# Rows of about one KB in the loads, and 32 stationary columns on four column groups in the products of a with the state

## The chip, the cores and the metric

The kernel runs on one NeuronCore of a Trainium2 chip. The metric is device time in microseconds: the median of several executions, and beside it one execution that was taken with the hardware profiler. TensorE's engine is PE in the views (PEld is its weight loads), VectorE is DVE, ScalarE is ACT, GpSimd is POOL, SyncE is SP. Most transfers are issued by SP's queue, in the order in which they stand there.

## The reference, cut to what matters

```python
# r, k, v, w, a, b: (4, 8, 768, 40) float32; state: (4, 8, 40, 40)
for t in range(768):
    y[:, :, t] = einsum('bhd,bhde->bhe', rt, state)
    Sa = einsum('bhde,bhe->bhd', state, at)
    state = state * wt[:, :, None, :] - einsum('bhd,bhe->bhde', Sa, bt) + einsum('bhd,bhe->bhde', vt, kt)
x = y, as (4 * 768, 320)
h = maximum(x @ w_in, 0);  x = (h * h) @ w_out               # 320 -> 2048 -> 320
g = x @ w_gate;  x = (g / (1 + exp(-g)) * (x @ w_val)) @ w_out   # 320 -> 1536 -> 320
```

The five weight matrices come as float64.

## The kernel before, in words

The recurrence is done in chunks of 32 steps (`C`), 24 chunks per batch. A group g (48 of them) is one chunk of two batches, that is 16 (batch, head) states, eight on partitions 0 to 39 and eight on 64 to 103 (of 104, `EPAD`). `e_stage` (lines 761 to 790) loads a group's w, a, k and b (`WA`, printed as wakb or room) and builds decay products with scans on DVE; `x_stage` multiplies a and b products inside a chunk; `inverse` solves the triangular systems of a window of four groups with 30 small DVE operations, after its input went through DRAM (`xi`); `chain` (lines 924 to 1006) carries the state from chunk to chunk, in 24 steps of stages named u, s and t; `slot` (lines 1015 to 1092) makes the output y from k, c, z, S and y stages. Four slots are one block of 256 rows for the first MLP (`pair1`), whose products (lines 461 and 466, each float32 matrix as a high and a low fp32r part) run between the stages of the recurrence. The second MLP follows when the recurrence is over, after about 750 us.

The stage u sums two things in one PSUM bank: 32 products with 32 stationary columns (line 955), then 16 products of a with the state (line 961), each with 64 stationary columns that hold the two halves q of a, and 40 moving columns of the state:

```python
for p in range(2):
    s = 4 * (n % 2) + 2 * (n // 2) + p
    nc.tensor.matmul(quad(tag)[64 * p:64 * p + 64, u, n], AB[nas[u]][:, s].rearrange("e q t -> e (q t)"),
                     ST[u][:, s, 0:D], start=False, stop=u + n == 4)
```

TensorE is used in tiles (32x32, 64x64, 128x64, or the whole array); the planner calls that an operation's mode, and two of one mode may be put behind each other. Each of these float32 products stands in the trace as two records.

The weights of the first MLP are loaded by `conv` (lines 1237 to 1278) in 36 jobs through four buffers `cx` (one lies in the tile `room`), turned from float64 into float32 by ACT, DVE and POOL, and split. The last 64 of the 320 rows of w_in would fill only half the partitions, so four of the jobs (named hl jobs here) bring two column blocks of them at once, one onto partitions 0 to 63, one onto 64 to 127, in one transfer whose source is written with the block as its outermost dimension (lines 1169 to 1171):

```python
src = w[r0:r0 + 64, c.start:c.start + 512].rearrange("p (g n) -> g p n", g=2)
```

The order of the work on all engines is set when the program is built, by a planner (class `Plan`): every operation has a due time and a cost per engine, and the planner simulates the engines and writes each engine's instructions in the order of its simulation. While PE would be idle before 220 us of its own time, it puts in filler products (line 1288, tile `warm`). The order on an engine is fixed from then on, and an engine waits at each instruction for what it needs.

## Time and profile before

| | us |
|---|---|
| median of 3 executions | 1205.25 (1201.82 to 1207.41) |
| profiled execution, its own time | 1207.99 |
| its span, first to last instruction | 1206.2 |
| granted TensorE clock, mean over the span | 0.959 of full speed |
| PE busy | 1115.2 |

The span falls into a front of about 205 us in which the weights are brought in and the recurrence starts, a dense part to about 755 us in which the recurrence and the first MLP share PE, and the second MLP. The profiled execution is 2.74 us above the median. A time in a row is counted from the span's start.

### The profile page before, as it was taken

How to read it: one execution, taken by the hardware profiler on the slowest of the kernel's cores; microseconds unless marked ns; L12 is line 12 of the kernel's file. 1: busy time of each engine (PE TensorE's matmuls, PEld its weight loads, DVE VectorE, ACT ScalarE, POOL GpSimd, SP SyncE). 2: the span in 40 equal slices, each digit the busy share in tenths (PEclk: the TensorE clock that was granted, in tenths of full speed). 3: DMA queues.
4: the chain of work that ended last, by engine and by line, in shares of the span. 5: the costliest groups of instructions: out<-in, count | busy, mean ns of one | idle time of the engine just before them, and what ended most of it. 6: DMA issues, size and time to landing. Idle time of an engine off the chain costs nothing.

```text
span 1206.2 us, 42916 instructions
## 1 busy us (share of the span) xinstructions
PE 1115.2 (92%) x18622; PEld 1016.1 (84%) x18622; DVE 643.8 (53%) x1551; ACT 550.0 (46%) x1296; POOL 93.3 (8%) x118
## 2 busy tenths in 40 slices
PE   7486987999899998999898999999999999999997
PEld 6475877889898997989797989988888888888886
DVE  4775876666575574856464422355444343434433
ACT  6344875555465464655454445563322222222221
POOL 0221332001110101110000000000000000000000
PEclk9688888999899998999899999999999999999998
DMA  5645555555566565654243321533101010010000
GB/s 136 152 122 161 151 161 140 128 155 150 146 161 175 129 166 127 171 143 116 83 104 80 76 66 44 142 97 90 32 12 27 22 27 23 20 29 1 22 1 26
DMA packets 171394, 114.97 MB, mean 95 GB/s; under 512 B 104092, under 2 KB 147644, under 8 KB 171196
## 3 DMA queue, kind: packets, MB, share of 16 engines
q1 hardware_dynamic: 168470, 110.62, 35.1%
q8 instruction: 148, 2.42, 0.8%
q10 hardware_dynamic: 2726, 1.51, 0.5%
q14 instruction: 50, 0.41, 0.1%
HBM read 88.35 MB, written 23.72 MB: 93 GB/s over the span
## 4 chain that ended last, share of the span: by engine, by line
PE 78%; DMA 7%; DVE 5%; issue 4%; SPq 3%; ACT 2%; POOL 0%; DVEq 0%; ACTq 0%
PE ps L461 33%; PE ps L466 13%; PE ps L1479 10%; SPq L724 3%; PE ps L1058 3%; PE ps L1030 2%; PE ps L1039 2%; PE ps L961 2%; PE ps L803 2%; DMA ws<-f_moe_w_val 2%; PE ps L1073 2%; PE ps L1000 2%; PE ps L974 2%; PE ps L869 1%; PE ps L955 1%
## 5 line engine op out<-in xcount | busy, mean ns | idle before, releaser
L1471 DVE TENSOR_TENSOR gr<-ps,gr 128x512 f32<-128x512 f32 x144 | 99.5, 691 | 165.9 <-PE ps L461 84.3
L1152 ACT ACTIVATE ps<-ps 128x512 f32<-128x512 f32 x192 | 111.6, 581 | 108.8 <-PE ps L461 106.7
L466 PE MATMUL ps<-o1h,gh 128*128 128x320 f32 x384 | 132.9, 346 | 3.6 <-ACT gh L436 3.6
L466 PE MATMUL ps<-o1h,gl 128*128 128x320 f32 x384 | 123.2, 321 | 1.6 <-DVE gl L413 1.4
L436 ACT CAST gh<-gr 128x512 fp32r<-128x512 f32 x72 | 44.7, 621 | 174.1 <-DVE gr L1471 173.7
L466 PE MATMUL ps<-o1l,gh 128*128 128x320 f32 x384 | 121.9, 318 | 0.0
L461 PE MATMUL ps<-xh,w1h 128*128 128x256 f32 x384 | 117.9, 307 | 0.0
L461 PE MATMUL ps<-xl,w1h 128*128 128x256 f32 x384 | 110.9, 289 | 0.1
L461 PE MATMUL ps<-xh,w1l 128*128 128x256 f32 x384 | 110.6, 288 | 0.0
L1479 PE MATMUL ps<-o2h,gl 128*128 128x320 f32 x288 | 89.1, 309 | 0.1
L1479 PE MATMUL ps<-o2l,gh 128*128 128x320 f32 x288 | 88.9, 309 | 0.2 <-DVE o2l L1395 0.2
L1479 PE MATMUL ps<-o2h,gh 128*128 128x320 f32 x288 | 88.8, 308 | 0.2 <-ACT o2h L436 0.2
L413 DVE TENSOR_TENSOR gl<-ps,gh 128x512 fp32r<-128x512 f32 x96 | 65.5, 682 | 34.2 <-ACT gh L436 33.7
L466 PEld LDWEIGHTS ps<-o1h,gh 128*128 128x128 f32 x384 | 74.8, 195 | 8.0 <-ACT gh L436 4.5
L1468 ACT ACTIVATE gr<-ps 128x512 f32<-128x512 f32 x72 | 43.2, 600 | 80.9 <-PE ps L461 79.4
L466 PEld LDWEIGHTS ps<-o1h,gl 128*128 128x128 f32 x384 | 75.0, 195 | 4.1 <-DVE gl L413 3.9
L461 PEld LDWEIGHTS ps<-xh,w1h 128*128 128x128 f32 x384 | 75.2, 196 | 1.7
L461 PEld LDWEIGHTS ps<-xl,w1h 128*128 128x128 f32 x384 | 75.5, 197 | 0.4 <-DVE xl L1101 0.3
L466 PEld LDWEIGHTS ps<-o1l,gh 128*128 128x128 f32 x384 | 75.4, 196 | 0.1
L461 PEld LDWEIGHTS ps<-xh,w1l 128*128 128x128 f32 x384 | 75.0, 195 | 0.0
L1133 DVE TENSOR_TENSOR gl<-gr,gh 128x512 fp32r<-128x512 f32 x72 | 49.9, 693 | 46.8 <-ACT gh L436 46.8
L1288 PE MATMUL ps<-warm 128*128 128x256 f32 x284 | 48.8, 328 | 22.1 <-DVE ct L1219 13.9
(171 smaller groups left out, 2711.4 us busy)
## 6 DMA issues: line engine op xcount, KB each, us to landing
wakb<-in_wakb_dram SPq DMA_DIRECT2D x42, 422.5 KB
RB<-in_vr_e_dram SPq DMA_DIRECT2D x46, 208.0 KB
RH<-in_r_e_dram SPq DMA_DIRECT2D x90, 80.0 KB
cx<-in_moe_w_out_dram SPq DMA_DIRECT2D x21, 320.0 KB
room<-xt_d SPq DMA_DIRECT2D x36, 128.0 KB
cx<-in_moe_w_in_dram SPq DMA_DIRECT2D x15, 256.0 KB
xt_d<-yb SPq DMA_DIRECT2D x24, 160.0 KB
x_d<-room SPq DMA_DIRECT2D x24, 160.0 KB
```

The source lines that it names most:

```text
L413: nc.vector.tensor_sub(dst, full, hi.bitcast(F32))
L436: nc.scalar.copy(dst, src) if e == ACT else eng[e].tensor_copy(dst, src)
L461: nc.tensor.matmul(ps, w[:, c], x, start=(i == 0), stop=(i == len(seq_) - 1))
L466: nc.tensor.matmul(acc[t][:, :DM], g[:, half, ts], w[:, f, :], start=(f == 0 and i == 0), stop=(f == nf - 1 and i == 2),)
L724: o = att(cost, lambda e: queues[e].dma_start(dst(), src()), r, w, due=due, dma=dma, tag="dma")
L1058: nc.tensor.matmul(v[64 * q:64 * q + D, p, s], w, x, start=not kb, stop=bool(kb))
L1133: op({POOL: t_pool(512), DVE: t_dve(512)}, lambda e: eng[e].tensor_sub(gl[n], two["gr"][n], gh[n].bitcast(F32)), (("gr", n), ("gh", n)), ( ...
L1152: op({ACT: 0.478}, lambda e, f=f: nc.scalar.activation(P1[b], P1[b], f), (), (("p", b),), due=due, tag="relu")
L1288: nc.tensor.matmul(PS[:, b, 0:256].rearrange("p (a b) -> p a b", a=2), warm, warm[:, None, :].to_broadcast([128, 2, 128]), start=True, sto ...
L1468: op({ACT: 0.478}, lambda e: nc.scalar.activation(both(two["gr"]), two["pg"][b], AF.Sigmoid), (("pg", b),), (("gr", n),), tag="sig", **kw)
L1471: op({DVE: 0.602}, lambda e, q=q: nc.vector.tensor_mul(both(two["gr"]), two[q][b], both(two["gr"])), ((q, b),), (("gr", n),), tag="u" + q, ...
L1479: nc.tensor.matmul(ACC2[t][:, :DM], x[n][:, t // 2, c], y[:, f, :], start=(f == 0 and i == 0), stop=(f == nf - 1 and i == 2))
```

## The change

Four things are changed.
- In the stage u, each product of a with the state is cut in two: 32 stationary columns (one q) instead of 64, so 32 products instead of 16 per step, on four column groups of the array. The planner is told a cost of 1.0 instead of 1.35 for the stage, and that it leaves the array in 128x32 mode.
- The tiles into which wakb, RB, RH and cx are loaded get a gap of two elements between rows of about 1 KB, so that a row of 2 to 4 KB lands as two to four rows. For groups from 4 on, wakb, until now one transfer of 1040 columns, is now two (272 columns, and 3 x 256).
- The hl jobs' loads are now two transfers of 64 partitions each, without the outer dimension of two.
- The identity matrix is loaded into the tile UQ and copied by ACT into one fp32r tile that serves the fillers and the transposes.

```diff
+GAP = 2
-    ident = keep.tile([128, 128], F32, name="ident")
+    warm = keep.tile([128, 128], F32R, name="ident")
+    ident = warm.bitcast(F32)
...
+    def in_halves(x, n):
+        return x.rearrange("p (k c) -> p k c", k=2)[:, :, 0:n // 2]
...
-    nwa = NWA + 24 * C
+    row = 8 * C + GAP
+    nwa = NWA + 3 * row
...
+    ncx = DM + GAP if wide_ else DM
+    cx = ring(cv, NCX - 1, [128, ncx], a["moe_w_in"].dtype, "cx")
...
-    RH = ap_.tile([EPAD, 2, 8, C], F32, name="RH")
+    RH = ap_.tile([EPAD, 2, row], F32, name="RH")
-    RB = ap_.tile([EPAD, 2, 8, C], F32, name="RB")
+    RB = ap_.tile([EPAD, 2, row], F32, name="RB")
...
+    def rows(t):
+        return t[:, NWA:].rearrange("p (n x) -> p n x", n=3)[:, :, 0:8 * C]
...
-        if g < HEAD:
-            load(lambda: WA[wa(g)][:, 0:NWA], lambda: a["wakb"][data(g)][:, 0:NWA], (), (kw,), due - 1, 0.5)
-            load(lambda: WA[wa(g)][:, NWA:], lambda: a["wakb"][data(g)][:, NWA:], (), (ka0, ka1, kk), due - 1, 1.35)
-        else:
-            load(lambda: WA[wa(g)], lambda: a["wakb"][data(g)], (), (kw, ka0, ka1, kk), due - 1, 1.8)
+        load(lambda: WA[wa(g)][:, 0:NWA], lambda: a["wakb"][data(g)][:, 0:NWA], (), (kw,), due - 1, 0.5)
+        load(lambda: rows(WA[wa(g)]), lambda: a["wakb"][data(g)][:, NWA:].rearrange("e (n t) -> e n t", n=3), (), (ka0, ka1, kk), due - 1, 1.35)
...
-                    for p in range(2):
-                        s = 4 * (n % 2) + 2 * (n // 2) + p
-                        nc.tensor.matmul(quad(tag)[64 * p:64 * p + 64, u, n], AB[nas[u]][:, s].rearrange("e q t -> e (q t)"),
+                    for k in range(4):
+                        s = 4 * (n % 2) + 2 * (n // 2) + k // 2
+                        nc.tensor.matmul(quad(tag)[32 * k:32 * k + 32, u, n], AB[nas[u]][:, s, k % 2],
                                          ST[u][:, s, 0:D], start=False, stop=u + n == 4)
...
-        stage("u", i, 1.35, u_mm, ...
+        stage("u", i, 1.0, u_mm, ...
-              mode="32x32", leaves="128x64", act=1840)
+              mode="32x32", leaves="128x32", act=1840)
...
-                    src = w[r0:r0 + 64, c.start:c.start + 512].rearrange("p (g n) -> g p n", g=2)
-                    yield src, 256, ...
+                    yield [w[r0:r0 + 64, c.start + 256 * g:c.start + 256 * (g + 1)] for g in range(2)], 256, ...
...
-        op({SP: 0.45}, lambda e: nc.sync.dma_start(x[:, :n], src), (),
-           kxs + [names["l"]], due=due - 1, dma=n * 1024 / 240e3, tag="dW")
+        some = [(x, src)] if not isinstance(src, list) else [(x[64 * g:64 * g + 64], y) for g, y in enumerate(src)]
+
+        def fetch(e):
+            for d, y in some:
+                nc.sync.dma_start(in_halves(d, n) if wide_ else d[:, :n], in_halves(y, n) if wide_ else y)
+
+        op({SP: 0.45 * len(some)}, fetch, (), kxs + [names["l"]], due=due - 1, dma=n * 1024 / 240e3, tag="dW")
...
-    load(lambda: ident, lambda: a["ident"], (), ("ident",), -29, 0.2)
+    eye = UQ.rearrange("p u i d -> p (u i d)")[:, 0:128]
+    load(lambda: eye, lambda: a["ident"], (), ("uq",), -29, 0.2)
```

The order of the instructions moves with this. SP's queue at the first weight jobs, before (cx is the buffer of a weight job, the third row is the first hl job; xi is the input of the first window's inverse; wakb and room are the groups 4 to 7):

```order
L1245 DMA cx_114<-in_moe_w_in_dram 128x256
L1245 DMA cx_115<-in_moe_w_in_dram 128x256
L1245 DMA cx_116<-in_moe_w_in_dram 128x1x256
L724 DMA xi<-xi_d_60 64x16x16 x2
L724 DMA wakb_166<-in_wakb_dram 104x1040
L724 DMA wakb_167<-in_wakb_dram 104x1040
L1245 DMA cx_114<-in_moe_w_out_dram 128x320
```

and now:

```order
L1254 DMA cx_114<-in_moe_w_in_dram 128x2x128
L1254 DMA cx_115<-in_moe_w_in_dram 128x2x128
L1254 DMA cx_116<-in_moe_w_in_dram 64x2x128 x2
L730 DMA xi<-xi_d_60 64x16x16 x2
L730 DMA wakb_166<-in_wakb_dram 104x272
L730 DMA wakb_166<-in_wakb_dram 104x3x256
L730 DMA wakb_167<-in_wakb_dram 104x272
L730 DMA wakb_167<-in_wakb_dram 104x3x256
```

The places are the same; the hl job is two transfers, and each wakb is two. Up to the end of the recurrence and the weights, SP's queue holds 967 transfers instead of 925.

SP's queue at the second hl job, before (room<-xt_d is the first block's input, p1t and P are results of the inverse):

```order
L724 DMA room<-xt_d_64 128x256 x2
L724 DMA room<-xt_d_64 128x1x256
L724 DMA p1t<-p_d_67 16x512 x2
L724 DMA P_128<-pt_d_63 32x2x128 x4
L724 DMA P_129<-pt_d_63 32x2x128 x4
L724 DMA qt<-in_eye_dram 128x256
L1245 DMA room<-in_moe_w_in_dram 128x1x256
```

and now:

```order
L1254 DMA room<-in_moe_w_in_dram 64x2x128 x2
L1254 DMA cx_115<-in_moe_w_out_dram 128x2x160
L730 DMA room<-xt_d_64 128x256 x2
L730 DMA room<-xt_d_64 128x1x256
L730 DMA p1t<-p_d_67 16x512 x2
L730 DMA P_128<-pt_d_63 32x2x128 x4
```

The hl job has moved ahead of the block's input.

PE's queue at the eighth step of the chain, before (L955 and L961 are the stage u; L803 is an x stage, in 128x64 mode):

```order
L955 MATMUL ps<-TV_158,L_121 32x40 x16
L955 MATMUL ps<-TV_158,L_122 32x40 x16
L961 MATMUL ps<-ST_151,AB_144 64x40 x8
L961 MATMUL ps<-ST_152,AB_145 64x40 x8
L803 MATMUL ps<-AB_149,KB_131 64x64 x8
```

and now:

```order
L961 MATMUL ps<-TV_158,L_121 32x40 x16
L961 MATMUL ps<-TV_158,L_122 32x40 x16
L967 MATMUL ps<-ST_151,AB_144 32x40 x16
L967 MATMUL ps<-ST_152,AB_145 32x40 x16
L1079 MATMUL ps<-ident,ST_151 104x104 x4
```

Before, six of the 24 steps had a stage of the same mode behind them; now none has. Over the whole program PE changes its mode 423 times instead of 407, and 296 filler products stand in its queue instead of 284.

## Rows read from the trace of the kernel before

**Rows 1.** The page's busy time by engine.
```profile
PE 1115.2 (92%) x18622; PEld 1016.1 (84%) x18622; DVE 643.8 (53%) x1551; ACT 550.0 (46%) x1296; POOL 93.3 (8%) x118
```

**Rows 2.** Windows: stretch, length, busy by engine, granted clock, DMA share, GB/s.
```profile
0.00:205.00 205.00, 153.08 (x3417) 139.15 (x3418) 141.26 (x374) 123.78 (x332) 48.04 (x65) 0.85 0.57 147
205.00:755.00 550.00, 521.96 (x12809) 486.03 (x12808) 312.65 (x867) 283.46 (x685) 42.46 (x50) 0.97 0.48 123
...
800.00:1206.00 406.00, 397.10 (x2089) 349.80 (x2087) 170.94 (x269) 114.32 (x216) 2.77 (x3) 0.99 0.10 28
```

**Rows 3.** PE's groups by line and form: busy us, mean ns of one record.
```profile
L961 PE MATMUL ps<-ST,AB 104*64 104x40 f32 x768 | 27.2, 230 | 0.0
```

**Rows 4.** Timeline, PE's stages near 335 us: start, length, line, records.
```profile
332.37 0.85 PE L1000 MATMUL ps<-TV,KT 64*40 64x40 f32 x64
...
333.15 0.69 PE L1039 MATMUL ps<-RB,RW 104*64 104x64 f32 x16
...
339.39 0.79 PE L955 MATMUL ps<-TV,L 32*32 32x40 f32 x64
...
340.11 1.13 PE L961 MATMUL ps<-ST,AB 104*64 104x40 f32 x32
...
341.07 0.67 PE L803 MATMUL ps<-AB,KB 104*64 104x64 f32 x16
```

**Rows 5.** Chain of waits, one step of line 961 with the whole array behind it.
```profile
255.20 1.06 PE ps L961 x32
```

**Rows 6.** Weight loads of lines 955 and 961: ns shortest/median/longest.
```profile
L955 PEld LDWEIGHTS ps<-TV,L x1536: 101/107/112, 19.4 to 717.7; 32*32 32x32 f32 x192
...
L961 PEld LDWEIGHTS ps<-ST,AB x768: 132/138/138, 20.1 to 718.7; 104*64 104x64 f32 x192
```

**Rows 7.** Timeline of SP's queue from 25 to 36 us.
```profile
25.57 1.56 SPq L1245 DMA_DIRECT2D cx<-in_moe_w_in_dram  x3
27.25 4.43 SPq L724 DMA_DIRECT2D xi<-xi_d  x2
31.77 3.31 SPq L724 DMA_DIRECT2D wakb<-in_wakb_dram  x2
```

**Rows 8.** Windows as in rows 2, by what the transfers were.
```profile
30.00:35.00 5.00, 0.32 (x3) 0.12 (x1) 0.90 (x3) 0.42 (x3) 0.73 (x1) 1.00 0.27 57
36.00:44.00 8.00, 0.39 (x2) 0.39 (x3) 7.04 (x33) 1.32 (x4) 0.31 (x1) 0.50 0.87 226
...
125.00:129.00 4.00, 4.00 (x84) 3.84 (x81) 3.06 (x7) 3.56 (x9) 2.33 (x3) 0.68 0.14 47
...
755.00:800.00 45.00, 43.03 (x313) 41.10 (x313) 18.95 (x42) 28.49 (x64) 0.00 (x0) 1.00 0.43 124
```

**Rows 9.** Chain of waits, the three longest pieces of the front.
```profile
27.94 7.69 DMA xi<-xi_d
...
109.19 8.87 DMA room<-in_moe_w_in_dram
...
160.59 8.61 DMA RH<-in_r_e_dram
```

**Rows 10.** Chain of waits, a later load of xi.
```profile
611.46 3.96 DMA xi<-xi_d
```

**Rows 11.** Timelines of DVE and PE: idle time before an instruction, in brackets.
```profile
35.73 0.17 DVE L833 TENSOR_TENSOR tmp<-qt,xi 128x15 f32<-128x15 f32 x1 [4.80 <-DMA xi<-xi_d]
...
120.22 0.70 PE L803 MATMUL ps<-AB,KB 104*64 104x64 f32 x16 [3.92 <-DVE ct L1219]
```

**Rows 12.** Waits by engine: us in total, times, longest.
```profile
PE ps L1058 <- DMA RH<-in_r_e_dram: 2.4, 1, 2.4
```

**Rows 13.** SP's issues of wakb (ns shortest/median/longest), and the chain's shares by engine.
```profile
L724 SPq DMA_DIRECT2D wakb<-in_wakb_dram x46: 307/372/2894, 2.1 to 643.2; - x46
...
PE 78%; DMA 7%; DVE 5%; issue 4%; SPq 3%; ACT 2%; POOL 0%; DVEq 0%; ACTq 0%
```

**Rows 14.** Timeline of PE, fillers in the front.
```profile
21.18 9.14 PE L1288 MATMUL ps<-warm 128*128 128x256 f32 x74
```

## The prediction

> **What bounds the kernel now.** I read the busy times first, then the windows, then the chain of waits, and last the timelines where the change bites. PE is busy for 92% of the span [rows 1], but not evenly [rows 2]: in the dense part, from 205 to 755 us, it is busy 522 of 550 us, in the second MLP 397 of 406, and in the front 153 of 205, where part of the busy time is fillers (one run of 74 of them takes 9.14 us [rows 14]). So there are two ways to shorten this kernel: fewer PE nanoseconds in the dense part, which count in full, or shorter waits in the front, which count as far as the next wait is not right behind. The change does one of each.

> The reader should look at two places. The first is line 961, the products of a with the state: 768 records, 27.2 us busy [rows 3], 32 records in each of 24 steps. In the timeline they start at 340.11 and the next stage at 341.07 [rows 4], 0.96 us or 30 ns per record; line 955 just ahead starts 64 records of the same 40 columns from 339.39 on, in 0.72 us, 11.2 ns each. Where the whole array follows instead of a stage of the same mode, a step of line 961 takes 1.06 us [rows 5].

> The second is the hl jobs. SP issues the first one last of three at about 26.6 us, and xi right behind it at 27.25 [rows 7]. xi lands 7.69 us after the issue of its second half [rows 9], where a later one takes 3.96 [rows 10]. In the middle of that, from 30 to 35 us, the 16 DMA engines are busy for 0.27 and move 57 GB/s, and from 125 to 129 us, after the third hl job, for 0.14 at 47 GB/s; the wakb loads that follow the first hl job reach 0.87 and 226 GB/s from 36 to 44 us [rows 8]. A share of 0.14 is 2.2 engines of 16: a transfer whose source begins with a dimension of two runs on about two engines. Its 256 KB need 262/47 = 5.6 us so, and 262/226 = 1.2 us at the rate of the wakb loads. Everything issued behind it that touches those two engines waits. [...]

> **The change, part by part.**

> *The stage u.* 16 products with 64 stationary columns become 32 with 32, so 64 records of 40 moving columns per step. No row before shows four column groups fed from the same 104 partitions, so I bound it. From above in speed: line 955 has the same count, columns and stationary width, 0.72 us. The weight loads do not forbid it: a load takes 107 ns with 32 columns and 138 with 64 [rows 6], 31 ns for 32 columns; 64 columns thus need some 62 ns, and yet line 961 starts a record every 30, so the two column groups load at the same time, and four would need 31/4 = 8 ns a record, less than 11.2. From below: if only two of the four overlap, the pace stays 30 ns and a step takes 1.92 us (rival C). Nearest is a stage of 64 records with 40 columns in four tiles, line 1000, 0.78 us from 332.37 to 333.15 [rows 4]; I take 0.76, between it and 0.72. That saves 0.30 us on 1.06, in 24 steps **-7.2 us**, all on PE's own path (best end 0.72: -8.2). [...]

> *Modes.* A stage of line 803 or 1039 behind line 961 came without a change of mode (0.96 against 1.06), in six of 24 steps; now the u stage always pays one. Over the program there are 16 more changes at that 0.10 us: **+1.6 us**. The 12 extra fillers stand in the front where PE waits; at 9.14/74 = 0.12 us each they cost 1.5 us only if the waits they fill are gone.

> *The hl jobs.* Each now spreads like the other loads. First: xi from 7.69 to a later one's 3.96, -3.7; DVE sat idle 4.80 us for it [rows 11], and the inverse, the p1t stage and the chain's first step follow DVE, so nothing else covers this. Second: its landing is a link of 8.87 us in the chain [rows 9], but PE worked through most of that, and only its idle of 3.92 us before line 803, which the conversion of this job ended [rows 11], comes back: -3.9. It also moves ahead of the block's input xt; at 1.2 us of transfer that delays it by no more than it gains. Third: PE is busy all through 125 to 129 us [rows 8]; nothing. Fourth: RH lands 8.61 us after issue because it stands behind it [rows 9]; PE's wait for RH was 2.4 us [rows 12], -2.4. Together **-10.0 us**, the bound if nothing waits right behind; the other bound is 0 (rival B). [...]

> *Rows of one KB.* The bytes stay. At 226 GB/s with 0.87 of 16 engines, a busy engine moves 16.2 GB/s with rows of 4 KB; from 755 to 800 us, where rows are 1 to 1.3 KB, 124/(16 x 0.43) = 18.0 [rows 8]. That is 10% of the transfer time, on loads that are issued groups ahead of use. The dense part has DMA shares of 0.48, so engines have room: 0 on the path, up to -8.4 (rival A).

> *More issues.* SP holds 42 transfers more, each 0.372 us of its queue [rows 13], 15.6 us. SP's queue makes 3% of the chain, 36 us, out of some 925 x 0.372 = 344 us of issues, so about a tenth of them is on the path: **+1.6 us** (0 to 4). They stand ahead of TV, RB and xi in the same queue, which is where a loss would show. The scan of a group now waits for 272 columns instead of 1040, a gain too small to price. The identity by way of ACT has its copy before as well, for the fillers: nothing.

> **The sum:** -7.2 + 1.6 - 10.0 + 1.6 = -14.0, from the profiled execution's 1207.99 to 1194.0. That execution lies 2.74 above the median of the runs, so on the runs' scale **1191 us**.

> **Rivals.**
> - **A, the rows are worth more.** The 44 wakb loads of 423 KB take 1.9 us each at 226 GB/s, 84 us; a tenth of it is 8.4 us. For it: small loads (P, p1t, xi, TV) stand behind wakb in the same queue and end waits; DMA is 7% of the chain [rows 13]. Against: the share of 0.48. It gives 1183.
> - **B, the front does not give.** What follows the hl jobs is conversions on ACT and DVE (busy 124 and 141 of 205 us [rows 2]) in a fixed order; if these are late next, the faster transfers only lengthen waits elsewhere. Then -7.2 + 1.6 + 1.6 = -4.0: 1201, no difference to be told. [...] What speaks against B itself is that DVE's 4.80 us and PE's 3.92 us ended just when these transfers or their conversion did.
> - **C, slower: the four column groups do not overlap.** They read the same rows of the array's partitions, and every four-tile stage above spreads over several row groups. If records start every 30 ns as in line 961 now, a step costs 64 x 30 = 1.92 instead of 0.96 us, +23.0 in 24 steps, and with +1.6 + 1.6 - 10.0 the kernel takes 1221. At 15 ns per record the term is nought; above about 19 ns (24 steps losing the 6.8 that the rest saves) the whole change loses. Against: two column groups visibly load at the same time.

> **How the numbers follow.** The forecast 0.60, A 0.10, B 0.18, C 0.12. The bound of what can be told is 0.5%, 6 us: faster is under 1199.2, slower over 1211.3. The forecast is faster in nearly all of its spread (0.56 of 0.60), A wholly, B in about a third, since part of 10 us can come through; C is slower but for a partial form. Faster 0.72, no difference 0.18, slower 0.10. The range, **1180 to 1207**, takes in A with the best end of u, B and a u that gains nothing, and leaves out C.

> **What would show it.** Right: the 64 records of the new line start within 0.72 to 0.80 us; the first xi lands within about 4 us of its issue; no stretch after an hl job's issue shows a DMA share near 0.14 at some 50 GB/s; PE's idle time of the front falls by some 8 to 10 us and the dense part begins that much earlier; the stretch behind it is shorter by 4 to 6 us. Wrong: records that start 15 ns or more apart (C); the same front with DVE or ACT as the releaser of the waits (B); wakb at 226 GB/s as before would rule out A; longer waits of PE for TV, RB or xi would mean that the added issues cost more than their tenth.

## The result, and the profile after

The changed kernel takes 1217.77 us (median of 8 runs, 1210.71 to 1223.41) against 1203.38 (8 runs, 1197.78 to 1207.87) of the kernel before on the same chip: ratio 1.0114, 95% interval 1.0078 to 1.0151. It is slower by 1.1%; the forecast was 1191, faster by 1.2%.

Line numbers have moved: what was 955, 961, 862, 974 and 1058 before is 961, 967, 868, 980 and 1064 after. First the windows of the changed kernel (columns as in [rows 2]), the two under the dots behind two hl jobs, of which the third is now issued at 118.1 us instead of 123.4:

```profile
0.00:205.00 205.00, 155.75 (x3408) 140.94 (x3408) 138.47 (x367) 122.15 (x328) 49.46 (x66) 0.85 0.58 148
205.00:755.00 550.00, 512.77 (x13455) 472.04 (x13454) 316.79 (x871) 281.58 (x680) 42.57 (x51) 0.97 0.49 123
...
30.00:35.00 5.00, 2.87 (x13) 2.87 (x14) 3.71 (x17) 1.93 (x6) 1.46 (x2) 0.50 0.89 209
120.00:125.00 5.00, 4.46 (x147) 3.88 (x135) 1.99 (x5) 3.79 (x11) 1.32 (x2) 1.00 0.82 227
```

The transfers did what they were to do: DMA shares of 0.27 and 0.14 [rows 8] have become 0.89 and 0.82. DVE's wait for the first xi is 0.85 us instead of 4.80 [rows 11], and the inverse starts 4.2 us earlier:

```profile
31.57 0.17 DVE L839 TENSOR_TENSOR tmp<-qt,xi 128x15 f32<-128x15 f32 x1 [0.85 <-DMA xi<-xi_d]
```

Yet PE is idle for 37.2 of the 550 us of the dense part, 9.2 more than before [rows 2]. The waits of PE from 60 to 755 us (total, times, longest) tell where:

```profile
PE ps L868 <- DMA p1t<-p_d: 12.9, 6, 5.3
PE ps L967 <- issue: 10.1, 5, 3.0
PE ps L1064 <- issue: 5.6, 4, 2.3
PE ps L471 <- issue: 5.1, 2, 2.8
PE ps L980 <- issue: 4.2, 6, 1.2
```

The wait for p1t is not the answer: it is 10.6 us in a kernel with the same order that does not lose (the sixth run below). The stage u itself is as fast as forecast. In PE's timeline of the changed kernel, 64 records start at 392.36 and the next stage at 393.09, 0.73 us; before it was 1.06 [rows 5]. But one step earlier the same stage stands still in its middle for 2.98 us, after 27 of its 64 records, and the releaser is "issue": nothing that the profile shows was awaited.

```profile
358.48 0.47 PE L967 MATMUL ps<-ST,AB 104*32 104x40 f32 x27
361.93 0.58 PE L967 MATMUL ps<-ST,AB 104*32 104x40 f32 x37 [2.98 <-issue]
...
392.36 0.80 PE L967 MATMUL ps<-ST,AB 104*32 104x40 f32 x64
393.09 0.42 PE L471 MATMUL ps<-o1h,gh 128*128 128x320 f32 x1
```

### The profile page after: what moved, and what is told of

It reads as the page before. It is cut to its first block, busy times and chain, and to the rows that moved or that the text cites. A ratio compares the mean times of both kernels' runs of the same rounds, so it can differ in the third digit from the quotient of the medians.

```text
span 1220.4 us, 44593 instructions
## 1 busy us (share of the span) xinstructions
PE 1120.6 (92%) x19402; PEld 1013.1 (83%) x19402; DVE 647.4 (53%) x1552; ACT 549.8 (45%) x1293; POOL 94.8 (8%) x120
## 4 chain that ended last, share of the span: by engine, by line
PE 68%; DMA 6%; issue 3%; SPq 3%; DVE 2%; ACT 1%; DVEq 0%; ACTq 0%
PE ps L466 31%; PE ps L471 11%; PE ps L1490 10%; SPq L730 2%; PE ps L1064 2%; PE ps L1045 2%; DMA ws<-f_moe_w_val 2%; PE ps L1036 1%; PE ps L1079 1%; PE ps L809 1%; PE ps L980 1%; PE ps L1006 1%; PE ps L967 1%; DMA xi<-xi_d 1%; PE ps L868 1%
## 5 line engine op out<-in xcount | busy, mean ns | idle before, releaser
L1299 PE MATMUL ps<-ident 128*128 128x256 f32 x296 | 50.2, 329 | 20.0 <-DVE w1l L1239 7.6
```

Of the source, the lines that this page charges most:

```text
L1299: nc.tensor.matmul(PS[:, b, 0:256].rearrange("p (a b) -> p a b", a=2), warm, warm[:, None, :].to_broadcast([128, 2, 128]), start=True, sto ...
```

## The experiments

Every ratio is to the kernel before, run beside it on the same chip. The first theory was that the loss is the planner's other order ("order"); the first rival, that it is the split loads ("transfers"). I call the 32 products of 32 columns narrow and the 16 of 64 columns wide.

**Four ways to put order and transfers apart.** The first kernel is the one before with the narrow products emitted and the planner's numbers left, so that each engine's order is unchanged.

```diff
-for p in range(2):
-    s = 4 * (n % 2) + 2 * (n // 2) + p
-    nc.tensor.matmul(quad(tag)[64 * p:64 * p + 64, u, n], AB[nas[u]][:, s].rearrange("e q t -> e (q t)"), ...
+for k in range(4):
+    s = 4 * (n % 2) + 2 * (n // 2) + k // 2
+    nc.tensor.matmul(quad(tag)[32 * k:32 * k + 32, u, n], AB[nas[u]][:, s, k % 2], ...
```

> The kernel before with the 32 narrow products of the stage u and nothing else; the planner keeps its numbers for u, so every engine's order is that of the kernel before. Theory 'order' (the loss of the change is the different static order that the planner writes): -7.2 us from 24 steps and +0.6 for six steps that now change the mode, some 1197 us, ratio 0.993 to 0.996, and no new idle time of PE. Theory 'transfers' (the loss comes from the split and added loads in SP's queue): the same 1197. Third, that the narrow products themselves cost time elsewhere (the stage that follows, weight loads): 1204 or more.

Measured: 1224.54 us, ratio 1.0144 (1.0109 to 1.0180). The narrow products alone, in the old order and with the old loads, lose more than the whole change. Both theories fall; the third case of the expectation holds.

The second is the whole change with the planner's old numbers (both transfers of a wakb in one operation, whose function `pair` issues them, and those of an hl job at the cost of one):

```diff
-load(lambda: WA[wa(g)][:, 0:NWA], ...)
-load(lambda: rows(WA[wa(g)]), ...)
...
+o = att({SP: 0.42}, pair, (), (kw, ka0, ka1, kk), due=due - 1, dma=1.8, tag="dma")
...
-stage("u", i, 1.0, ..., leaves="128x32", ...)
+stage("u", i, 1.35, ..., leaves="128x64", ...)
...
-op({SP: 0.45 * len(some)}, fetch, ...
+op({SP: 0.45}, fetch, ...
```

> The whole change, but with the planner's numbers of before: u at its old cost and mode, the two transfers of a wakb in one operation, an hl job's two at the cost of one. Each engine's order is that of the kernel before; only SP's queue holds the added transfers. Theory 'order': -14 us as forecast, 1190 us, ratio 0.985 to 0.992. Theory 'transfers': slower than before like the change, 1212 to 1218, ratio above 1.005, with the same waits for p1t, P and xi as in the change.

Measured: 1218.76, 1.0110 (1.0065 to 1.0156): by the numbers the case of "transfers", but with the run above it is the narrow products again.

The third is the first with the planner's new numbers for u; the fourth is the changed kernel with the old ones.

```diff
-stage("u", i, 1.35, ..., leaves="128x64", ...)
+stage("u", i, 1.0, ..., leaves="128x32", ...)
...
-stage("u", i, 1.0, ..., leaves="128x32", ...)
+stage("u", i, 1.35, ..., leaves="128x64", ...)
```

> The kernel before with the narrow products and the planner's new numbers for u (cost 1.0, leaves 128x32), loads untouched; the order differs on every engine. Theory 'order': worse than the same products in the old order, by 5 to 15 us, so 1202 to 1212 us, with PE idle ahead of u as in the change. Theory 'transfers': no worse than in the old order, 1197 us.

> The changed kernel with the planner's old numbers for u (cost 1.35, leaves 128x64), the products narrow, all loads as changed. Theory 'order' with u's numbers as the cause: 1195 to 1205 us, 1 to 2 per cent under the change. If the order is spoiled by the loads' own numbers (two operations for a wakb), or theory 'transfers' holds: as the change, 1213 to 1221.

Measured: 1219.44, 1.0124 (1.0091 to 1.0158), no worse than the first run; and 1208.47, 1.0038 (1.0008 to 1.0067), 9 us under the change. So the planner's numbers shift the time by up to 0.8%, in one base and not in the other.

**What "issue" is.** The page lists one more queue, with packets, MB and share. The kernel before, then the changed one:

```profile
q8 instruction: 148, 2.42, 0.8%
```

```profile
q8 instruction: 154, 2.52, 0.9%
```

Each packet is 2.42 MB / 148 = 16 KB. PE has 18622 records before, each a weight load and a product, 37,244 instructions; by 148 packets that is some 252 a packet, and the table below shows steps of 256. The narrow products add 768 records, 1536 instructions, and 1536/256 = 6 packets: 154. So PE's code is brought in during the run: in the kernel before, 124 of the 148 packets begin between 55 and 760 us. I then worked out, from the trace's records of this queue and of PE's instructions, where PE stood in its code at the end of a wait. Some of the waits over 0.8 us of the first run (narrow, old order):

```
wait of PE, us     long   before  instructions  packets    begun -      packet    wait ends
from      to       us     line    begun         landed     256xlanded   lands at  us later
 70.25     72.63   2.38   1058     1986           6        450            71.20   1.44
207.89    210.43   2.54    869     7106          26        450           208.92   1.51
239.02    240.32   1.30    961     8641          32        449           238.93   1.40
265.33    267.35   2.02    803    10177          38        449           265.95   1.40
315.62    319.38   3.76    869    12481          47        449           318.13   1.25
439.27    440.79   1.51   1000    18369          70        449           439.36   1.43
544.23    548.03   3.80    869    23746          91        450           546.54   1.48
718.44    719.63   1.19    974    31937         123        449           718.19   1.44
```

(Landed counts the packets before the one that ends the wait.) PE stood still at one place: in this table always 449 or 450 instructions past 256 times the packets landed, and it went on 1.25 to 1.51 us after the next had landed. Of the waits over 0.3 us between 55 and 760 us that end so soon after a packet (1.2 to 1.65 us), 35 of 36 stand on such a border in this run, 25 of 27 in the changed kernel, 17 of 18 in the kernel before; in the kernel before and the changed one PE began no instruction beyond that border in the whole span. Picked by their place instead, 78 waits of the three runs stand on a border, and every one ends 1.25 to 1.7 us after a packet has landed. The timeline of the first run shows one of them, again in the middle of u:

```profile
238.33 0.70 PE L961 MATMUL ps<-ST,AB 104*32 104x40 f32 x53
...
240.32 0.33 PE L961 MATMUL ps<-ST,AB 104*32 104x40 f32 x11 [1.30 <-issue]
```

The theory is that PE waits there for the next packet of its code. PE's waits for issue from 60 to 755 us add up to 32.9 us before and 34.4 after the change.

**Four tests of this theory ("code").** The changed kernel with the stage u undone altogether; the changed kernel in its own order, with only the 16 wide products emitted in place of the 32; the kernel before with 16 extra products of one moving column ahead of each stage u, into columns that nobody reads; and the kernel before with all the changed loads, in its old order, and the wide products. The first, second and fourth put back the three lines of the first diff above, on the changed kernel with the old numbers for u, on the changed kernel, and on the second run's; the third has this:

```diff
+for u in range(2):
+    for j in range(8):
+        k = j % 4
+        nc.tensor.matmul(bank(tag)[32 * k:32 * k + 32, 320:321], AB[nas[u]][:, j, 0], ST[u][:, j, 0:1], start=True, stop=True)
```

> The changed kernel with the stage u as before (16 products of 64 columns, the planner's old numbers), all loads as changed. Theory 'code', formed after the first four runs: PE's instructions come in packets of 16 KB, 256 instructions each, on the queue that the profile calls instruction; the narrow products add 64 instructions to each of 24 steps, six packets, and PE, which stands still for 'issue' exactly at a packet's border, loses some 24 us to them against the 6.6 they save. Then this kernel is some 17 us under the one with narrow products and old planner's numbers: 1188 to 1200, ratio 0.985 to 0.995. Theory 'order' (the loads' own numbers in the planner spoil the order): 1204 or more.

> The changed kernel in its own order, the planner's new numbers for u and all, but 16 products of 64 columns emitted instead of 32 of 32. Theory 'code': 17 us less than the change although u itself takes longer, 1196 to 1206, ratio 0.992 to 1.000, and fewer waits of PE for issue. Theory 'order': the order is the loss, so 1213 or more, like the change or, with u's longer step, 7 above it.

> The kernel before, in its order, with 16 extra products of one moving column at the start of each stage u, written to columns of the bank that nobody reads: as many instructions more as the narrow products bring (64 a step), with the wide products kept. Their own time on PE is at most 0.31 us a step, 7.4 us. Theory 'code': 20 us or more over before, 1224 to 1240, ratio above 1.014, and six more packets on the instruction queue. Rival, that 32-column products on four column groups disturb what follows in u: at most the 7.4, so 1207 to 1214, ratio under 1.007.

> The kernel before, in its order, with the changed loads and the stage u as it was. The second run (whole change in the old order) lay 5.8 us under the first (narrow products alone). Theory 'code': the loads are worth as much here, 1197 to 1203, ratio 0.992 to 0.998. Theory 'transfers' (rival: the split loads delay small ones): 1207 or more.

Measured: 1202.11, ratio 0.9959 (0.9934 to 0.9984), faster than before; 1210.25, 1.0002 (0.9976 to 1.0028); 1230.58, 1.0180 (1.0137 to 1.0222); 1207.79, 0.9984 (0.9958 to 1.0011). The third lies inside the range that I had given for "code"; the other three lie just over its upper ends (0.995, 1.000 and 0.998) and below what their rivals asked for in the first two (1204 and 1213 us). The fourth does not rule its rival out: 1207.79 is over its 1207, and the ratio is not told from 1. The runs now make four pairs that differ in the emitted products of u alone:

| order and loads | wide | narrow | narrow costs, us of 1208.8 | PE's waits for issue, 60 to 755 us, wide and narrow |
|---|---|---|---|---|
| old order, old loads | 1 | 1.0144 | 17.4 | 32.9 and 43.3 |
| old order, new loads | 0.9984 | 1.0110 | 15.2 | 22.2 and 38.4 |
| the change's order, new loads | 1.0002 | 1.0114 | 13.5 | 15.7 and 34.4 |
| planner's old numbers for u, new loads | 0.9959 | 1.0038 | 9.5 | 23.9 and 33.2 |

In each the narrow products lose, 13.9 us in the mean, and the waits for issue grow, by 13.7 us in the mean (the waits are of one profiled run each, and those runs lie only 10.4 us apart in the mean). At line 967 itself, with the change's order in both (PE and its weight loads together; us, times), the narrow and then the wide kernel:

```profile
  issue: 21.1, 11
```

```profile
  issue: 0.3, 1
```

The extra products confirm the size (21.8 us, of which their own time in the timeline, 446.33 to 446.70, is 0.37 x 24 = 8.9) but not the place: their q8 has 154 packets too, yet the waits for issue rise only to 37.1. What is left went into PE's busy time, at a lower granted clock (mean over the span 0.948 against 0.959 before). Its span and clock, and the page's busy times:

```profile
core 0: 1230.6 us, clock 0.948
```

```profile
PE 1137.3 (92%) x19390; PEld 1036.5 (84%) x19390; DVE 643.1 (52%) x1551; ACT 550.3 (45%) x1296; POOL 93.5 (8%) x118
```

1137.3 is 22.1 over before [rows 1], 13.2 more than the products' own time. The clock's share is of that size. What it withheld, one minus the mean, times the span, is 0.052 x 1230.6 = 64.0 us against 0.041 x 1206.2 = 49.5 before, 14.5 more (an estimate, as if PE were busy throughout). And between 200 and 755 us most falls of the granted clock came where PE had waited for code. In the kernel before, the trace's clock records show six stretches at 0.50 that begin between 200 and 755 us, and all six begin during a wait at a packet's border or at most 1.6 us after it. In the first run five of seven do, in the changed kernel five of seven, here eight of nine. One of them here, and the same time in the kernel before (columns as in [rows 2]):

```profile
203.74 0.62 PE L869 MATMUL ps<-P,vt 32*32 32x16 f32 x33 [2.93 <-issue]
...
204.00:216.00 12.00, 12.00 (x258) 10.90 (x251) 5.67 (x19) 3.20 (x8) 0.88 (x1) 0.50 0.42 110
```

```profile
204.00:216.00 12.00, 12.00 (x319) 11.04 (x318) 8.22 (x27) 6.11 (x15) 0.88 (x1) 0.91 0.39 105
```

So this wait for code cost its 2.93 us and, at the lower clock, slower work behind it: the products of line 466 start 0.27 us apart there (205.46 to 207.32) against 0.15 at a clock of 1.00 (390.71 to 391.15 of the kernel before). The four pairs go the same way: the granted clock, averaged over the runs, is lower with the narrow products in each (0.954 against 0.962, 0.961 against 0.965, 0.955 against 0.961, 0.960 against 0.965 in the table's order). By the same estimate that withholds 7.5 us more in the mean. With 13.7 us of waits it makes 21.2, as much as the 13.9 net and the 7.2 saved in u. That the clock fell because of the waits, and not of the products, is argued from where the stretches begin; no run varied it alone.

**Can the order give the code time to arrive?** The planner got a budget: an instruction takes 16.8 ns of it, some credit is kept, and a stage that would overdraw it yields to a product of the MLP, two instructions for 0.12 to 0.15 us of PE (from start to start, lines 461 and 466 near 391 to 394 us of the kernel before).

```diff
+def code_of(self, o, t):
+    n = o.cols // 128 if o.cols else CODE.get(o.tag[0], 8) if o.mode or o.take else 8
+    return max(self.code, t - CODE_AHEAD) + n * CODE_US
...
+if not o.cols and self.code_of(o, t) > t + o.cost[PE]:
+    return next((q for q in ok if q.cols), o)
...
+self.code = self.code_of(o, t)
+d = max(d, self.code - t)
...
+CODE = dict(u=192, s=128, t=128, v=128, p=128, y=128, x=32, c=32, z=16, k=8, S=8)
+CODE_US, CODE_AHEAD = 0.0168, 2.5
...
+CODE_US, CODE_AHEAD = 0.0168, 3.0
...
+CODE_US, CODE_AHEAD = 0.015, 2.5
```

The three settings are those of the first, the second, and the last two of the next four runs; in the last u counts 256.

> The kernel before with a planner that counts PE's instructions: each one takes 16.8 ns of a code budget with 2.5 us of credit, a stage that would overdraw it yields to a product of the MLP (two instructions for 0.1 us) if one is ready, and waits otherwise. No instruction is added or taken away. Theory 'code': PE stands at packet borders for less than half of the some 30 us that it does in the kernel before, and the kernel gains 8 to 20 us, ratio 0.983 to 0.993. Rival: the order that was tuned is lost and the chain of states gets late, 1207 or more, ratio above 1.000.

> The same code budget (16.8 ns, 3.0 us of credit) in the kernel with the changed loads and the wide products. Theory 'code': 8 to 20 us under that kernel's 1202, so 1182 to 1194, ratio 0.977 to 0.988 to the kernel before. Rival: 1202 or more.

> As the run before it with a milder budget (15 ns an instruction, 2.5 us of credit): between that run and the kernel without a budget if the budget is what helps, 1186 to 1200.

> The whole change (narrow products, planner's old cost for u, changed loads) with the milder budget, in which u counts 256 instructions. Theory 'code': the narrow products still bring six packets more; where products of the MLP stand between them they cost less than the 14 us of the earlier pairs, so 0 to 10 us over the run with wide products and the same budget. If the narrow products are then worth their 0.31 us a step: 7 us under it.

Measured, in this order: 0.9972 (0.9940 to 1.0004), 1.0000 (0.9969 to 1.0031), 0.9975 (0.9939 to 1.0011), 0.9952 (0.9915 to 0.9988). The waits for issue fell as foreseen, to 6.5, 6.1, 10.5 and 17.3 us, but the time did not follow. The first lies between its two expectations, the second and third are misses for "code". The fourth lies between its two cases: the whole change with narrow products is 0.2% under the third of these four, its wide partner (the intervals overlap), and 1.6% under the change as it was made. The orders of these two differ, since u counts 256 in the one and 192 in the other, so it is no fifth pair at a fixed order. In the first, waits of another kind had come in:

```profile
PE ps L880 <- DVE o1l L1245: 10.0, 1, 10.0
PE ps L814 <- DVE P L891: 5.2, 1, 5.2
```

The longer one lies in the front, at 117 us. So three more runs got the budget (with 3.0 us of credit) from 180 us of the planner's time on:

```diff
 def code_of(self, o, t):
+    if t < CODE_FROM:
+        return t
...
+CODE_FROM = 180.0
```

> The kernel before with the code budget (16.8 ns an instruction, 3.0 us of credit) from 180 us of the planner's time on, so that the front keeps its order; no instruction added or taken away. Theory 'code' (a wait at a packet's border costs its length): the waits of PE for issue behind 200 us, some 25 us in the kernel before, fall under 8, and the kernel gains 8 to 18 us, ratio 0.985 to 0.993. Rival (these waits lie where PE would wait for the chain of states anyway): within 4 us of the kernel before, ratio 0.997 to 1.003, with other waits in their place.

> The same late budget in the kernel with the changed loads and wide products, which took 1202 without it. Theory 'code': 1186 to 1196, ratio 0.981 to 0.990. Rival: 1199 to 1206, ratio 0.993 to 0.999.

> The same late budget in the whole change (narrow products, old cost of u), which took 1208.5 without it. Theory 'code': with MLP products between the small stages the six extra packets land in time and the narrow products keep most of their 0.31 us a step: 1186 to 1198, ratio 0.981 to 0.992. Rival (the extra packets cost the same in any order): 14 us over the run with wide products and the same budget.

Measured: 1201.13, 0.9928 (0.9893 to 0.9962); 1211.96, 1.0013 (0.9981 to 1.0046); 1228.31, 1.0146 (1.0094 to 1.0198). The first comes out as the theory had it in time, not in the size of the waits: no instruction is added or removed, the waits for issue fall from 32.9 to 14.4 us over 60 to 755 (behind 200 us from 27.5 to 10.8, where I had expected under 8), and the kernel is 0.7% faster than the one before, the fastest of all that I ran. Its order is new as well, so the run does not show that the waits alone gave this. The other two fail, though their waits for issue fall as well (23.9 to 13.2, 33.2 to 20.8). The last lies 16 us over the one before it, near the 14 of its rival, by which the packets cost the same in any order, but these two orders differ as well. In the last PE is busy only 506.34 us from 205 to 755, and waits for ACT, DVE and p1t stand in the place.

```profile
PE ps L882 <- DMA p1t<-p_d: 9.0, 5, 3.6
PE ps L1050 <- ACT TV L1004: 6.7, 3, 3.8
...
PE ps L485 <- DVE gl L429: 5.5, 4, 2.7
```

With the same products and loads, the narrow ones and the changed ones, five orders lie between 0.9952 and 1.0146 here, so a wait that an order removes need not come back as time.

## Why the prediction was wrong

The measured +13.8 us (1.14% of 1208.8) split over the kernels: the changed loads in the planner's own order -5.0 (0.9959), the planner's new numbers for u on top +5.2 (1.0002; the two intervals touch), the narrow products on top +13.5 (1.0114).

- **The step that failed is "-7.2 us, all on PE's own path".** The duration was right: 0.73 us undisturbed, 0.76 forecast, and rival C, with its 1.92, fell with it: 64 records on four column groups and the same 104 partitions started within those 0.73 us. What the step left out is that the added instructions had to be brought in, by 154 packets instead of 148. The stage went from 192 to 256 instructions, and its price was taken as its busy time. In the mean of four pairs the narrow products cost 13.9 us net of the gain, so some 21 us gross (adding 24 steps of 0.30): 13.7 us of waits at the borders of packets and, by estimate, 7.5 us at a lower granted clock. The chain's "issue 4%" [rows 13] was in front of me and got no price. Asking what those 4% were would have led to the packets, and to the question of what 1536 more instructions do.
- **Slower had 0.10, and only by rival C.** The loss came by a mechanism that was on no list; the range to 1207 did not hold the result.
- **The -10.0 us of the hl jobs failed too: the transfers went as forecast, the time did not.** Share and landing were right, PE's wait of 3.92 us before line 803 is gone, and that for RH is 0.7 us instead of 2.4. But PE's idle time of the front fell by 2.7 us (51.9 to 49.3), not by 8 to 10, since other waits grew. That for p1t before 205 us, first in the kernel before, then in the changed one:

```profile
PE ps L862 <- DMA p1t<-p_d: 4.3, 1, 4.3
```

```profile
PE ps L868 <- DMA p1t<-p_d: 7.8, 2, 5.3
```

  Of its bounds, 0 and -10.0, the forecast took the second, and no run shows it: the -10.0 became -1.9 in the old order (0.9984, not told from none) and -5.0 in the planner's own. That is rival B. The starts of u in each kernel against the kernel before (us, each from one profiled run) show how far the gain lives:

```
u in the kernel before       72    137    208    255    278    340    452    569    718
new loads, old order       -3.5   -5.6   -4.7   -4.6   -0.6   -0.9   +1.9   +4.2   +2.3
narrow alone, old order    -3.2   +3.4   +8.6   +8.9  +13.5  +14.7  +18.9  +20.1  +19.2
the change                 -3.5   +2.2  +10.2  +13.8  +12.8  +18.4  +21.7  +18.9   +9.2
```

  With the loads alone 4 to 5 us stand until 255 us and are gone at 278. Some 3 us of them can be scatter: narrow alone, whose loads are the old ones, begins the first of these steps 3.2 us early as well, and the run with extra products 3.7. What takes them at 278 wasn't tried; from 247 to 280 us PE's granted clock is 0.90 there against 0.95 before, and PE is idle for 3.3 us against 2.3. With the narrow products the loss is made between 72 and 450 us, where the stages of the recurrence are thickest among the MLP's work.
- **The order was taken as it stood.** The planner's cost for u fell by 0.35 us where PE's own time fell by 0.33 (1.06 to 0.73). The order that came of it lengthened the kernel in one base (+9.2 us between the fourth run and the change) but not in the other (third run against the first).
- **Modes, issues, rows of one KB** (+1.6, +1.6, 0) were not measured one by one. All of what the loads bring is within the -1.9 and -5.0, so rival A's 1183 is out; the rate of the wakb loads, by which it was to be judged, was not read.

## What to carry to other kernels

Count instructions as well as busy time. Where a profile says "issue", look at the instruction queue's packets and at whether the waits stand on their borders; the change here cut products into smaller ones for a faster stage and paid for each new instruction some 21 us / 1536 = 14 ns (by the estimate above), against 7.2 us / 1536 = 5 ns that it saved. Look also at the granted clock behind such waits. Test such a change with the order held fixed: orders alone moved the kernel with the whole change by 1.9% (0.9952 to 1.0146), more than either part of the change did at a fixed order.

## What the runs showed of the hardware

```profile
391.64 0.79 PE L961 MATMUL ps<-TV,L 32*32 32x40 f32 x64
```

- Behind such waits the granted clock fell to 0.50: all six stretches at that level that begin between 200 and 755 us in the kernel before began during one or at most 1.6 us after it, five of seven in the first run and five of seven in the changed kernel. Behind one wait of 2.93 us (the extra products) it was 0.50 for 12 us in which PE was busy throughout.
- 32 products with 32 stationary columns on four column groups, all from the same 104 partitions, took 0.73 us (392.36 to 393.09, changed kernel), 11.4 ns a record, near the pace of line 955 (11.2 [rows 4]).
